# Where the columns of v are put in order: in the read of the matmul or in the copy out of PSUM

## The chip, the cores and the metric

One core of a Trainium2 chip. The metric is the device time of one execution in microseconds (us). In this kernel TensorE does its matmuls out of SBUF into PSUM; ScalarE and VectorE copy PSUM back to SBUF. In the profile PE is TensorE's matmul side, PEld its weight loads (they overlap: 98% and 85% of the span busy in the kernel before), ACT is ScalarE, DVE is VectorE, and L299 is line 299 of the kernel. "Stationary" is the operand that is loaded as weights, "moving" the one that is streamed past them.

## The reference, cut to what matters

```
q, k, v: (8 batches, 8 heads, 576 positions, 64)         fp32
kv  = einsum('bhsd,bhse->bhde', k, v)                     # 64 x 64 per batch and head
out = einsum('bhsd,bhde->bhse', q, kv)
x   = out / sqrt(mean(out^2, -1) + 1e-6) * g_norm          # then (4608, 512)
h   = x @ w_in (512 x 2048);  g = s * relu(h)^2 + b;  result = g @ w_out
```

The two large products at the end are nearly all of the work. The change concerns only `kv`, the k^T v product.

## The kernel before: the parts that matter here

The later part of the kernel wants the 64 columns of `kv` (index e of v) in the order "all e with e % 4 = 0, then 1, 2, 3". The kernel before gets this order for nothing in instructions: the moving operand of the matmul is v read every fourth element.

```
def kv_product(b):
    ps = [ps_t.tile([P, 2, D], FP32, name="kv_ps", tag="t") for _ in range(2)]
    for i in range(2):
        kv = kv_in.pop((b, i))
        for j in range(R):                     # R = 9
            for l in range(2):                 # l, r: the four 64x64 quarters of the array
                for r in range(2):
                    rows = slice(r * HB, r * HB + HB)
                    nc.tensor.matmul(
                        ps[r][l * HB : l * HB + HB, i, :].rearrange("p (c e) -> p c e", c=KC),
                        lhsT=kv[rows, 0, l, j, :],
                        rhs=kv[rows, 1, l, j, :].rearrange("p (e c) -> p c e", c=KC),
                        start=(j == 0), stop=(j == R - 1),
                    )
    for r in range(2):
        for l in range(2):
            ls = slice(l * HB, l * HB + HB)
            to = bd_kv[b % 2][ls, 2 * r : 2 * r + 2, ls]
            if b == 0 and l == 1:
                nc.vector.tensor_copy(out=to, in_=ps[r][ls])
            else:
                nc.scalar.copy(to, ps[r][ls])
...
```

(HB and D are 64, KC is 4.) So one batch is 2 x 9 x 2 x 2 = 72 calls of a 64 x 64 x 64 matmul and four copies of 64 x 128 elements. The traces hold two matmuls, each with its own weight load, for every such fp32 call: 144 a batch, 1152 in all. Matmuls are counted here as the traces count them, and the 144 of one batch are called a burst. Batch 0 is done at the start of the kernel, beside the first transfers; batches 1 to 7 are wedged one by one between the large matmuls.

## Time and profile before

| | before |
|---|---|
| time, median of the first 3 runs | 1001.62 us (1001.38 to 1002.2) |
| span of the profiled run | 1000.7 us |
| TensorE busy | 98% |
| k^T v matmuls (L299) on the chain that ended last | 3% |
| ScalarE, VectorE busy | 21%, 47% |

Read the chain first (which engine's work sets the end), then the groups of instructions by shape, then single bursts. The lines are in the prediction. One that it tells only in words is the copies after one burst, on ScalarE (columns: start us, duration us, engine, line, operation, operands, count, and in brackets the idle time before and who ended it):

```profile
176.25 1.07 ACT L313 COPY bd_kv<-kv_ps 64x128 f32<-64x128 f32 x4 [3.75 <-PE kv_ps L299]
```

The four copies start when the burst is over, and ScalarE had stood idle for 3.75 us by then: there is room for slower copies.

### The profile page before, as it was taken

Reading aid. Unit: us, or ns where it says so; the run is one execution under the profiler, and the core shown is the slowest. Engines: PE = TensorE matmul, PEld = TensorE weight load, DVE = VectorE, ACT = ScalarE, POOL = GpSimd, SP = SyncE. Lnnn points to the kernel's source line nnn. Section 1 sums busy time; section 2 is a strip of 40 time slices with the busy share of each in tenths; the row PEclk is TensorE's granted clock in tenths of the full one; section 3 lists DMA queues with packets and bytes.
Section 4 is the critical chain, followed back from the end, with each engine's and each line's share of the span. In section 5 each row is a group of like instructions: output and inputs, shape, how many; then the busy total and the mean of one; then the engine's idle time right before and its main releaser. Section 6 shows DMA issues by size and latency. Waiting matters only on the chain.

```text
span 1000.7 us, 15059 instructions
## 1 busy us (share of the span) xinstructions
PE 979.1 (98%) x6514; PEld 851.7 (85%) x6514; DVE 474.6 (47%) x777; ACT 208.7 (21%) x386; POOL 6.7 (1%) x18
## 2 busy tenths in 40 slices
PE   4999999999999999999999999999999999999998
PEld 3788888888888888888888888888888888888887
DVE  2689557453435444444345344533454444443441
ACT  2673131212220212121111212121112111212100
POOL 2000000000000000000000000000000000000000
PEclk9899999999999999999999999999999999999999
DMA  9688638522551344132442255125203240323033
GB/s 230 193 303 245 229 82 224 137 84 96 159 138 43 126 144 107 56 128 80 144 124 94 85 158 138 63 107 152 60 10 135 77 158 1 126 75 137 1 126 84
DMA packets 74225, 121.56 MB, mean 121 GB/s; under 512 B 41776, under 2 KB 47920, under 8 KB 66864
## 3 DMA queue, kind: packets, MB, share of 16 engines
q1 hardware_dynamic: 72208, 119.16, 39.0%
q10 hardware_dynamic: 1632, 1.44, 0.6%
q8 instruction: 51, 0.84, 0.3%
q14 instruction: 14, 0.11, 0.0%
q0 software_dynamic: 320, 0.00, 0.0%
HBM read 103.81 MB, written 16.78 MB: 121 GB/s over the span
## 4 chain that ended last, share of the span: by engine, by line
PE 94%; DVE 3%; DMA 2%; issue 0%; SPq 0%; ACT 0%; DVEq 0%; ACTq 0%
PE x_ps L84 48%; PE y_ps L84 30%; PE z_ps L84 8%; PE x_ps L345 3%; PE kv_ps L299 3%; PE qT_ps L331 1%; DMA kv_sb<-in_k_dram 1%; DMA q_sb<-in_q_dram 1%; DVE ws L186 1%; DVE xs L186 0%; DVE a L183 0%; DVE ws L183 0%; DVE a L437 0%; PE y_ps L345 0%; DVE wb L186 0%
## 5 line engine op out<-in xcount | busy, mean ns | idle before, releaser
L84 PE MATMUL x_ps<-w_sb,a 128*128 128x256 f32 x768 | 173.6, 381 | 0.0
L84 PEld LDWEIGHTS x_ps<-w_sb,a 128*128 128x128 f32 x768 | 144.6, 190 | 21.2 <-issue 2.8
L84 PE MATMUL y_ps<-w_sb,a 128*128 128x256 f32 x640 | 144.0, 381 | 0.0
L84 PEld LDWEIGHTS y_ps<-w_sb,a 128*128 128x128 f32 x640 | 120.3, 191 | 16.5 <-issue 1.4
L84 PE MATMUL x_ps<-xs,ws 128*128 128x256 f32 x512 | 121.2, 380 | 1.4 <-DVE ws L186 1.1
L84 PE MATMUL y_ps<-xs,wb 128*128 128x256 f32 x512 | 121.0, 380 | 0.0
L480 ACT COPY r<-x_ps 128x512 f32<-128x512 f32 x96 | 56.2, 585 | 298.3 <-PE x_ps L84 290.3
L84 PEld LDWEIGHTS x_ps<-xs,ws 128*128 128x128 f32 x512 | 97.4, 191 | 15.0 <-issue 1.5
L84 PEld LDWEIGHTS y_ps<-xs,wb 128*128 128x128 f32 x512 | 97.6, 191 | 13.0
L183 DVE TENSOR_TENSOR a<-y_ps,r 128x512 f32<-128x512 f32 x64 | 44.0, 688 | 122.1 <-ACT r L480 122.1
L84 PE MATMUL x_ps<-xT,wa 128*128 128x256 f32 x384 | 91.7, 387 | 0.0
L84 PEld LDWEIGHTS x_ps<-xT,wa 128*128 128x128 f32 x384 | 74.5, 195 | 10.8 <-ACT xT L384 0.4
L552 DVE SCALAR_TENSOR_TENSOR or<-x_ps,s_col,b_row 128x256 f32<-128x256 f32 x52 | 25.0, 483 | 94.5 <-PE x_ps L84 90.3
L437 DVE SCALAR_TENSOR_TENSOR a<-a 128x512 f32<-128x512 f32 x96 | 66.5, 692 | 3.3
L513 DVE TENSOR_TENSOR a<-a 128x512 f32<-128x512 f32 x32 | 22.1, 692 | 88.4 <-ACT a L512 88.4
L84 PE MATMUL x_ps<-xT,ws 128*128 128x256 f32 x256 | 61.1, 382 | 0.0
L84 PE MATMUL z_ps<-xT,wa 128*128 128x256 f32 x256 | 60.5, 380 | 0.0
L84 PE MATMUL x_ps<-w_sb,s 128*128 128x256 f32 x256 | 58.5, 382 | 0.0
L84 PEld LDWEIGHTS x_ps<-xT,ws 128*128 128x128 f32 x256 | 48.3, 190 | 7.3 <-issue 1.1
L84 PEld LDWEIGHTS z_ps<-xT,wa 128*128 128x128 f32 x256 | 48.8, 191 | 6.5
L84 PEld LDWEIGHTS x_ps<-w_sb,s 128*128 128x128 f32 x256 | 47.6, 190 | 7.2 <-issue 1.4
L356 DVE TENSOR_REDUCE ss<-xn 128x8 f32<-128x512 f32 x36 | 24.6, 684 | 52.9 <-ACT xn L354 52.2
(93 smaller groups left out, 855.8 us busy)
## 6 DMA issues: line engine op xcount, KB each, us to landing
w_sb<-w SPq DMA_DIRECT2D x56, 1024.0 KB, 4.9
out_dram<-o SPq DMA_DIRECT2D x72, 128.0 KB, 2.3
q_sb<-in_q_dram SPq DMA_DIRECT2D x70, 128.0 KB, 6.2
kv_sb<-in_k_dram SPq DMA_DIRECT2D x30, 288.0 KB, 5.1
kv_sb<-in_v_dram SPq DMA_DIRECT2D x30, 288.0 KB, 7.0
w_raw<-in_moe_w_in_dram SPq DMA_DIRECT2D x8, 1024.0 KB, 6.4
w_raw<-in_moe_w_out_dram SPq DMA_DIRECT2D x8, 1024.0 KB, 5.0
w<-w_up SPq DMA_DIRECT2D x3, 1024.0 KB, 6.9
```

The source lines that it names most:

```text
L84: nc.tensor.matmul(o, lhsT=lhsT, rhs=rhs, start=start, stop=stop, skip_group_check=True)
L183: nc.vector.tensor_tensor(out=o, in0=a, in1=b, op=ALU.add)
L186: nc.vector.tensor_tensor(out=o, in0=a, in1=b, op=ALU.subtract)
L299: nc.tensor.matmul(ps[r][l * HB : l * HB + HB, i, :].rearrange("p (c e) -> p c e", c=KC), lhsT=kv[rows, 0, l, j, :], rhs=kv[rows, 1, l, j, ...
L331: nc.tensor.transpose(ps[:, p, :], q_in[c][:, 2 * p : 2 * p + 2, :], ident)
L345: nc.tensor.matmul(ps[32 * p : 32 * p + 32, w, :], lhsT=st["qT"][:, p, 32 * w : 32 * w + 32], rhs=bd_kv[(b if w < 2 else b1) % 2][:, p, :] ...
L356: nc.vector.reduce_sum(st["ss"], st["xn"], axis=mybir.AxisListType.X)
L437: nc.vector.scalar_tensor_tensor(t, t, 0.0, t, ALU.max, ALU.mult)
L480: nc.scalar.copy(st[name], src)
L513: nc.vector.tensor_mul(t, t, t)
L552: nc.vector.scalar_tensor_tensor(o, ps, s_col, other, ALU.mult, ALU.add)
```

## The change

Its intent: let the matmul stream v as it lies in SBUF, and pay for the order where the result is small, in the copies that are made anyway.

```
                         nc.tensor.matmul(
-                            ps[r][l * HB : l * HB + HB, i, :].rearrange("p (c e) -> p c e", c=KC),
+                            ps[r][l * HB : l * HB + HB, i, :],
                             lhsT=kv[rows, 0, l, j, :],
-                            rhs=kv[rows, 1, l, j, :].rearrange("p (e c) -> p c e", c=KC),
+                            rhs=kv[rows, 1, l, j, :],
...
-                to = bd_kv[b % 2][ls, 2 * r : 2 * r + 2, ls]
+                to = bd_kv[b % 2][ls, 2 * r : 2 * r + 2, ls].rearrange("p i (c e) -> p i c e", c=KC)
+                src = ps[r][ls].rearrange("p i (e c) -> p i c e", c=KC)
                 if b == 0 and l == 1:
-                    nc.vector.tensor_copy(out=to, in_=ps[r][ls])
+                    nc.vector.tensor_copy(out=to, in_=src)
                 else:
-                    nc.scalar.copy(to, ps[r][ls])
+                    nc.scalar.copy(to, src)
```

## The prediction

The sum of the forecast came to 987.9 us: 1001.6 less seven bursts of 1.95 us (13.7 us). They are a paragraph that weighed such figures against the trace, the bound for the slower copies ("twofold" in rival 4 refers to it), and the paces that rivals 2 and 3 assumed, with the times worked out from them. The 0 for the copies stands as the author's estimate, from ScalarE's 21% and the 3.75 us that it idles in a burst. The upper end of the range, 998, was the time of rival 2, an assumption; the shift from 987.9 to 989 rests on the rivals likewise.

> **What bounds the kernel now.** I read the page from its head: busy shares, then the chain that ended last, then groups of instructions by shape, then the timeline around one k^T v product, and last the single records of that stretch.
>
> ```profile
> PE 979.1 (98%) x6514; PEld 851.7 (85%) x6514; DVE 474.6 (47%) x777; ACT 208.7 (21%) x386; POOL 6.7 (1%) x18
> PE 94%; DVE 3%; DMA 2%; issue 0%; SPq 0%; ACT 0%; DVEq 0%; ACTq 0%
> PE x_ps L84 48%; PE y_ps L84 30%; PE z_ps L84 8%; PE x_ps L345 3%; PE kv_ps L299 3%; PE qT_ps L331 1%; DMA kv_sb<-in_k_dram 1%; DMA q_sb<-in_q_dram 1%; DVE ws L186 1%; DVE xs L186 0%; DVE a L183 0%; DVE ws L183 0%; DVE a L437 0%; PE y_ps L3
> ```
>
> TensorE sets the time: 98% busy and 94% of the chain. The line that the change touches, L299, is 3% of the span (30 us) on that chain. This is the ceiling of the whole gain, before any mechanism.
>
> ```profile
> L345 PE MATMUL x_ps<-bd_kv,qT 128*32 128x128 f32 x1088 | 37.3, 278 | 1.6 <-DVE qT L334 1.1 <-DVE xn L364 0.5
> L299 PE MATMUL kv_ps<-kv_sb 64*64 64x64 f32 x1152 | 35.8, 293 | 10.2 <-DMA kv_sb<-in_v_dram 10.2
> L299 PEld LDWEIGHTS kv_ps<-kv_sb 64*64 64x64 f32 x1152 | 33.7, 157 | 12.6 <-issue 12.6
> L313 ACT COPY bd_kv<-kv_ps 64x128 f32<-64x128 f32 x30 | 7.7, 259 | 46.7 <-PE kv_ps L299 46.5
> ```
>
> A pair to notice: a matmul that streams 64 columns (L299) takes 293 ns, one that streams 128 columns (L345) only 278 ns. Half the columns should cost less.
>
> ```profile
> 171.50 0.38 PE L84 MATMUL x_ps<-xT,wa 128*128 128x256 f32 x1
> 171.81 4.41 PE L299 MATMUL kv_ps<-kv_sb 64*64 64x64 f32 x144
> 176.15 0.48 PE L84 MATMUL x_ps<-xT,ws 128*128 128x256 f32 x1
> ```
>
> One product is one burst of 144 matmuls, wedged between the large matmuls with no wait inside. First start to last start is 4.41 - 0.29 = 4.12 us, so 4.12/143 = 28.8 ns a matmul and 115 ns for a group of four, one in each 64x64 quarter of the array. In the single records the four start within about 20 ns, then nothing starts until about 115 ns after the first: each quarter is busy with its own stream, and issue isn't the limit.
>
> **How long should a stream of 64 columns be?** 16 of the 256-column matmuls take 3.45 us on the chain: 216 ns each, or 0.84 ns a column. The 128-column matmuls of L345 repeat on a column tile every 109 ns: 0.85 ns a column, with their own weight loads hidden. At that rate 64 columns take 54 ns, plus some 2 ns: 56. The trace shows 115, so 59 ns are unexplained, and the only thing peculiar to L299's moving operand is that v is read every fourth element (16 bytes apart). The strongest sign comes from batch 0, which ran before the clock had risen:
>
> ```profile
> L299 PEld LDWEIGHTS kv_ps<-kv_sb x144: 175/202/229, 8.6 to 14.7; 64*64 64x64 f32 x144
> L299 PE MATMUL kv_ps<-kv_sb x144: 290/293/367, 8.6 to 14.9; 64*64 64x64 f32 x144
> ```
>
> Against 129/151/154 and 290/291/306 for the burst at 171.8. The loads took 46 ns more at the minimum, roughly the 54 ns that a doubled stream of 64 columns would add, but the matmuls kept their 290 ns. I read it as half clock (the transposes that follow at 15.08 also come about 215 ns apart instead of 109; the page records no clock so early). A stream that doesn't slow when the array does isn't paced by the array but by its reads.
>
> [...]
>
> **The change, part by part.**
> - Removed: the strided read, in 8 x 144 = 1152 matmuls. The weights, the number of matmuls, the PSUM addresses written and the accumulation stay.
> - Array time after: 56 ns a group if the next weights load entirely beside the stream. A load of a 64-column weight also occupies about 53 ns (in the records the second group's loads follow the first's by 53 to 55 ns), and it begins 1 ns after the matmul whose slot it waits for. So loads and streams are now nearly equal in length and some friction is likely. I choose 62 ns, an estimate.
> - Per burst: 36 groups x (115 - 62) = 1.91 us, and the last matmul ends some 60 ns sooner, which shortens the hand-over to the next large matmul by perhaps that. Call it 1.95 us: 4.34 becomes about 2.4.
> - How many bursts count: batches 1 to 7 lie on the chain between large matmuls. Seven times 1.95 is 13.7 us. Batch 0 lies beside transfers, as the start of the chain shows:
>
> ```profile
> 2.44 8.87 DMA kv_sb<-in_k_dram
> 11.31 0.02 issue
> 11.32 0.58 SPq L135
> 11.90 0.04 issue
> 11.95 0.63 SPq L114
> 12.58 0.04 issue
> 12.62 8.68 DMA q_sb<-in_q_dram
> 21.30 0.14 issue
> 21.43 0.64 PE qT_ps L331 x4
> ```
>
> TensorE waits for q until 21.4 whatever batch 0 does at 8.6 to 15.1: gain 0.
> - Added: the stride in the copies out of PSUM. Same 32 instructions and bytes; [...] on an engine 21% busy, with no wait for bd_kv on ScalarE's copies anywhere in L345's idle time. For batch 0 two copies are on VectorE ahead of the copies of qT; [...] Cost on the path: 0.
> - Moved: TensorE reaches everything after each burst 2 us sooner. The one place where VectorE sets the pace, 148 to 168 us (the operand sums of the second unit), begins with a wait for TensorE at 147.6, so batch 1's gain passes through.
>
> Sum: 1001.6 - 13.7 = 987.9. I place the single number slightly up, at 989, because the rivals below all take from the gain.
>
> **Rivals.**
> 1. The stride isn't the cost; a weight load and a stream take turns in a quarter (54 + 54 + 7 = 115). For: the sum fits, and loads are stretched from 129 to 151 ns. Against: half clock would make it 215, and batch 0 shows 115 to 123. Time: 1001.6, no change.
> 2. Issue takes over: [...] For: no sustained rate above one in 27 ns is seen. Against: after a semaphore at 16.96 us the sequencer put out 13 loads and matmuls in 80 ns, 6 ns each, so a group of 8 would need 49. [...]
> 3. Loads and streams overlap badly once equally long[...]
> 4. The PSUM read is far slower than twofold, or VectorE or ScalarE becomes late for the next large group. Against: in each burst VectorE and ScalarE stop after their 0.5 to 0.7 us of leftovers and wait 3.75 us. Time: still under 1001.6 unless copies exceed 2 us each.
>
> **Range and chances.** Best case 56 ns a group and the short hand-over: 7 x (36 x 59 + 60) ns = 15.3 us, 986.3; runs before differed by 0.8 us. [...] So 8 in 10: 985.5 to 998. A gain over 2% needs 20 us off, more than two thirds of the 7 x 4.34 = 30.4 us that these bursts hold, a group in under 40 ns, shorter than its own stream; a loss over 2% needs a new wait of 20 us that nothing points to.
>
> **What would show it.** Right: L299's mean falls from 293 to about 220 ns (164 ns of fixed length, as in L345's 273 - 109, plus 56), the burst from 4.41 to about 2.5 us, its stretch on the chain from 3% to under 2%; large matmuls stay at 216 ns apart. Wrong by rival 1: the burst stays at 4.4. [...] By rival 4: [...]a new wait for bd_kv ahead of L345.

## The result, and the profile after

The changed kernel took 987.45 us (median of 4 runs, 986.9 to 988.22) against 1001.73 us (4 runs): ratio 0.9858, 95% interval 0.9841 to 0.9875. A ratio here is the mean time of one kernel's runs over the mean of the other's in the same rounds, so not quite the ratio of the medians. The gain is clear of noise and within 2%.

The page of the changed kernel (engines with busy us, share and instructions; then the chain by line):

```profile
PE 965.1 (98%) x6514; PEld 836.1 (85%) x6514; DVE 474.6 (48%) x777; ACT 208.8 (21%) x386; POOL 6.7 (1%) x18
PE x_ps L84 49%; PE y_ps L84 30%; PE z_ps L84 8%; PE x_ps L346 3%; PE kv_ps L299 2%; PE qT_ps L332 1%; DMA kv_sb<-in_v_dram 1%; DMA q_sb<-in_q_dram 1%; DVE ws L186 1%; ACT xT L385 0%; DVE xs L186 0%; DVE ws L183 0%; DVE a L183 0%; SPq L96 0
```

The same instructions in the same number; TensorE lost 14.0 us of busy time (15.6 us of its weight loads), the others none. On the chain L299 went from 3% to 2%. The groups by shape (busy us, mean ns, then idle before):

```profile
L299 PE MATMUL kv_ps<-kv_sb 64*64 64x64 f32 x1152 | 21.0, 231 | 10.8 <-DMA kv_sb<-in_v_dram 10.8
L299 PEld LDWEIGHTS kv_ps<-kv_sb 64*64 64x64 f32 x1152 | 19.7, 145 | 13.2 <-issue 13.2
L314 ACT COPY bd_kv<-kv_ps 64x128 f32<-64x128 f32 x30 | 7.7, 260 | 32.5 <-PE kv_ps L299 32.3
L312 DVE COPY bd_kv<-kv_ps 64x128 f32<-64x128 f32 x2 | 0.5, 290 | 0.7 <-ACT bd_kv L314 0.7
```

The matmuls' mean fell from 293 to 231 ns. The copies, which now read PSUM 16 bytes apart, take 260 ns against 259 on ScalarE and 290 against 290 on VectorE: the stride costs them nothing. The burst of batch 2 on the timeline:

```profile
169.69 0.38 PE L84 MATMUL x_ps<-xT,wa 128*128 128x256 f32 x1
170.00 2.35 PE L299 MATMUL kv_ps<-kv_sb 64*64 64x64 f32 x144
172.28 0.48 PE L84 MATMUL x_ps<-xT,ws 128*128 128x256 f32 x1
```

From the burst's first start to the first large matmul after it: 172.28 - 170.00 = 2.28 us, before 176.15 - 171.81 = 4.34.

Where the 14.3 us came from can be added up, because both traces hold the same matmuls in the same order. These are starts of the first large matmul after each burst (after batch 0, of the second group of 16), from the single records:

| after the burst of batch | before, us | changed, us | difference, us |
|---|---|---|---|
| 0 (second group of large matmuls) | 34.78 | 34.96 | +0.18 |
| 1 | 116.05 | 114.24 | -1.80 |
| 2 | 176.15 | 172.28 | -3.86 |
| 3 | 283.97 | 278.02 | -5.94 |
| 5 | 499.61 | 489.50 | -10.10 |
| 7 | 715.25 | 700.99 | -14.26 |
| last matmul of all | 995.95 | 981.69 | -14.26 |

Seven steps of 1.98 to 2.08 us, and nothing given back in the 280 us after the last burst. The first row is scatter of the start and no measure of batch 0: in after_again, the same kernel as the changed one, batch 1's burst starts at 110.53 us instead of 111.96. Counted from that burst's start to the last matmul the traces agree far better: 884.24 us before and 884.23 in only0, 869.72, 869.73 and 869.72 in the changed kernel, after_again and psum_write. The seven bursts are worth 14.51 us, 2.07 each.

### The profile page after: what moved, and what is told of

Its sections match the earlier page's. It is cut to its first block, busy times and chain, and to the rows that moved or that the text cites. A ratio compares the mean times of both kernels' runs of the same rounds, so it can differ in the third digit from the quotient of the medians.

```text
span 986.4 us, 15059 instructions
## 1 busy us (share of the span) xinstructions
PE 965.1 (98%) x6514; PEld 836.1 (85%) x6514; DVE 474.6 (48%) x777; ACT 208.8 (21%) x386; POOL 6.7 (1%) x18
## 4 chain that ended last, share of the span: by engine, by line
PE 93%; DVE 3%; DMA 2%; ACT 1%; issue 0%; SPq 0%; ACTq 0%; DVEq 0%
PE x_ps L84 49%; PE y_ps L84 30%; PE z_ps L84 8%; PE x_ps L346 3%; PE kv_ps L299 2%; PE qT_ps L332 1%; DMA kv_sb<-in_v_dram 1%; DMA q_sb<-in_q_dram 1%; DVE ws L186 1%; ACT xT L385 0%; DVE xs L186 0%; DVE ws L183 0%; DVE a L183 0%; SPq L96 0%; DVE xn L365 0%
```

## The experiments

They ran each on one chip, together with runs of the kernel before. "Spacing" is the time from one group of four matmuls to the next: four times (last start - first start)/143 in the burst of batch 3, from the single records. The records don't name the quarter of the array; that a group is one matmul in each quarter is read from the order of the calls.

| run | what is strided | spacing, ns | median, us | ratio to before (95%) |
|---|---|---|---|---|
| before | stream of v, 16 bytes | 115.2 | 1001.9 | |
| after_again | copies only | 59.0 | 987.7 | 0.9855 (0.9842 to 0.9869) |
| only0 | stream of v, batches 1 to 7 | 115.2 | 1002.06 | 0.9999 (0.9986 to 1.0011) |
| psum_write | write into PSUM | 59.0 | 987.69 | 0.9856 (0.9841 to 0.9871) |
| stride2 | stream of v, 8 bytes | 59.7 | 987.67 | 0.9856 (0.9842 to 0.9869) |
| stride8 | stream of v, 32 bytes | 116.4 | 1001.96 | 1.0001 (0.9984 to 1.0017) |
| half_plain | nothing, 32 columns | 58.2 | 986.93 | 0.9853 (0.9838 to 0.9867) |
| half_stride4 | stream of v, 16 bytes, 32 columns | 59.8 | 987.94 | 0.9862 (0.9847 to 0.9876) |
| k_strided | weights (k), 16 bytes | 118.6 | 1002.3 | 1.0006 (0.9991 to 1.0021) |

The theory under test: the matmul's stream was paced by reading elements 16 bytes apart. Its rivals: weight load and stream take turns; any gap costs; the cost only moves into PSUM; every burst counts alike.

**after_again.** The changed kernel, no edit.

> The changed kernel unchanged, for a tighter interval. All theories were made with its first result known: 987.5 us, ratio 0.986, bursts of 144 matmuls in 2.35 us.

Measured as expected; the interval of the ratio is now 0.9842 to 0.9869.

**only0.** Batch 0 alone is changed:

```
-                            rhs=kv[rows, 1, l, j, :],
+                            rhs=kv[rows, 1, l, j, :] if b == 0
+                            else kv[rows, 1, l, j, :].rearrange("p (e c) -> p c e", c=KC),
...      (the same choice for the place in PSUM and for the copies)
```

> Batch 0 alone reads v as it lies; batches 1 to 7 keep the strided read. Theory (batch 0 lies beside the transfer of q and counts nothing): within 0.1% of before, 1001.7 us, with the bursts of batches 1 to 7 at 4.4 us. Rival (every burst counts alike): one eighth of the gain, 1.8 us, about 999.9.

1002.06 us, ratio 0.9999. One eighth of the gain would be a ratio of 0.998, which lies outside the interval, 0.9986 to 1.0011, by a little. Batch 0 counts nothing that these runs can see: after it TensorE waits for q in both kernels (2.41 us before, 1.95 us in the changed one). The view by tile of batch 0 alone in only0 (weight loads, then matmuls; minimum/median/maximum ns, first and last start in us):

```profile
L299 PEld LDWEIGHTS kv_ps<-kv_sb x144: 175/223/228, 8.8 to 14.9; 64*64 64x64 f32 x144
L299 PE MATMUL kv_ps<-kv_sb x144: 311/311/364, 8.8 to 15.0; 64*64 64x64 f32 x144
```

This view also supports the prediction's reading of batch 0. Read as it lies, the stream takes 311 ns here and 218 ns later, so in these first 15 us the array is slow and a stream that the array paces is slow with it; the strided one was recorded at 290 ns in both places. That it was the clock is inferred, since the trace has no record of it there, from the kernel before: the transposes after batch 0 start 213 ns apart, and 110 ns apart from 16.41 us on, where the trace's first record of full clock begins (16.40). From 24.40 to 25.30 us, where the granted clock was 0.50, they start 213 ns apart again. By starts, which are measured and not modelled as the ends are: in the first 72 matmuls of batch 0, from the third group on, a group takes 115 to 121 ns before and 106 to 107 ns in only0; at full clock it takes 116 (before) and 58 (changed kernel). The slow clock nearly doubled the plain groups and hardly touched the strided ones.

**psum_write.** v is streamed as it lies, and the matmul's write into PSUM makes the order; the copies are the old ones:

```
-                            ps[r][l * HB : l * HB + HB, i, :],
+                            ps[r][l * HB : l * HB + HB, i, :].rearrange("p (c e) -> p e c", c=KC),
-                            rhs=kv[rows, 1, l, j, :],
+                            rhs=kv[rows, 1, l, j, :].rearrange("p (e c) -> p e c", c=KC),
...
-                src = ps[r][ls].rearrange("p i (e c) -> p i c e", c=KC)
+                src = ps[r][ls]
```

> v is read as it lies and the columns are put in order where the matmul writes PSUM (16 bytes apart in runs of 4 elements); the copies are those of before. Theory that only the read of v is slow: 987.5 us and 218 ns a matmul. Rival, [...]: groups of four near 115 ns, bursts near 4.4 us, about 1001.7 us.

(The distance in that text is wrong: consecutive results land 16 elements, 64 bytes, apart. The reason that it gave for the rival is cut: no run showed it.) The matmuls of one burst, in the view by tile:

```profile
L299 PE MATMUL kv_ps<-kv_sb x144: 218/218/267, 170.1 to 172.3; 64*64 64x64 f32 x144
```

The same as the changed kernel, in a correct result. A scattered write into PSUM is free here (59.0 ns a group with and without it), and so is the scattered read of the copies in the changed kernel (260 against 259 ns): the cost didn't move into PSUM, it went away. It was the read of SBUF alone. (A small slowing of the write could hide behind the weight load, but then the matmuls would be recorded longer, as in half_stride4 below; they kept 218 ns.)

**stride2 and stride8.** The stream of v every second, or every eighth element; the copies make up the rest of the order, so both results are correct.

```
 stride2
-                            ps[r][l * HB : l * HB + HB, i, :],
+                            ps[r][l * HB : l * HB + HB, i, :].rearrange("p (c e) -> p c e", c=2),
-                            rhs=kv[rows, 1, l, j, :],
+                            rhs=kv[rows, 1, l, j, :].rearrange("p (e c) -> p c e", c=2),
...
+                src = ps[r][ls].rearrange("p i (x h) -> p i h x", h=2)

 stride8: c=8 in the matmul, and
+                src = ps[r][ls].rearrange("p i (g c e) -> p i c e g", c=KC, g=2)
```

> v is read every second element (8 bytes apart[...]), the rest of the order is made in the copies; the result stays right. Theory [...]: groups at 58 ns, 987.5 us, as the changed kernel. Rival 1 (any gap between elements costs): groups at 115 ns, 1001.7 us. [...]

> v is read every eighth element (32 bytes apart); the result stays right. Theory [...] the same 115 ns a group, bursts of 4.4 us and 1001.7 us. Rival (cost grows with the distance): over 120 ns a group and over 1003 us.

(Cut from these two texts: the picture of what lies behind the cost, which no run showed, and a second rival to stride2 that rested on it.)

Two answers of the view by tile, the matmuls of one burst, stride2 and then stride8:

```profile
L299 PE MATMUL kv_ps<-kv_sb x144: 215/217/269, 169.5 to 171.7; 64*64 64x64 f32 x144
```

```profile
L299 PE MATMUL kv_ps<-kv_sb x144: 293/294/308, 171.5 to 175.7; 64*64 64x64 f32 x144
```

8 bytes apart costs what lying side by side costs (59.7 against 59.0 ns a group), 32 bytes apart costs what 16 bytes did (116.4 against 115.2). So it isn't "any gap", and hardly the distance: of the distances tried there is one step, between 8 and 16 bytes. What in the memory makes it was not shown.

**half_plain.** 32 of the 64 columns of v are streamed, weights as before. Its output is wrong, which doesn't matter for the time.

```
-                            ps[r][l * HB : l * HB + HB, i, :],
+                            ps[r][l * HB : l * HB + HB, i, : HB // 2],
-                            rhs=kv[rows, 1, l, j, :],
+                            rhs=kv[rows, 1, l, j, : HB // 2],
...                          (copies of 64 x 64)
```

> Wrong on purpose: only the first 32 columns of v are streamed, read as they lie; the weights keep their 64 columns. Which of the two paces a group at 58 ns now? If the weight load: groups stay at 55 to 58 ns, bursts near 2.3 us, about 987.5 us. If the stream: groups near 30 ns, bursts near 1.2 us, 7 x 36 x 28 ns = 7 us less, about 980.5 us.

The view by tile of one burst (weight loads, then matmuls; minimum/median/maximum ns):

```profile
L299 PEld LDWEIGHTS kv_ps<-kv_sb x144: 129/135/135, 169.3 to 171.4; 64*64 64x64 f32 x144
L299 PE MATMUL kv_ps<-kv_sb x144: 212/219/240, 169.3 to 171.4; 64*64 64x32 f32 x144
```

and the burst on the timeline:

```profile
169.28 2.33 PE L299 MATMUL kv_ps<-kv_sb 64*64 64x32 f32 x144
```

Half the stream, and the burst takes 2.33 us instead of 2.35: the stream no longer sets the pace. By the single records a slot of the group repeats every 58.3 ns in both kernels, with its parts differently placed: in the changed kernel a load starts 2 to 3 ns after the matmul before it and its matmul 56 ns later; in half_plain the load starts 30 ns after the matmul and its matmul 28 ns later. What stays is 58 ns from one load of 64 columns to the next, so the weight load is the likely pace-setter. No run has shorter weights, but three things speak for it: in the slow clock of batch 0 half_plain's groups take 107 ns, as 64 columns would at half speed (32 would take 54, an estimate from the 0.84 ns a column of the large matmuls); k_strided below makes the load longer and the group follows; and in the changed kernel nothing at all starts for 33 to 36 ns of each group of batch 3, so the issue of instructions isn't full.

**half_stride4.** 32 columns, every fourth element. Its output is wrong, which doesn't matter for the time.

```
+                            rhs=kv[rows, 1, l, j, :].rearrange("p (e c) -> p c e", c=KC)[:, :2],
...                          (32 places in PSUM; copies of 64 x 64)
```

> Wrong on purpose: 32 columns of v are streamed, every fourth element. Theory (the read of one element 16 bytes from the last takes about 1.77 ns and runs beside the weight load): 32 x 1.77 = 57 ns, groups at 57 to 60 ns, about 987.5 us. Rival 1 of the prediction (load and stream take turns, 54 + 27 + 7): 88 ns a group, about 995 us.

(The 1.77 ns are an estimate from the kernel before: 115.2 ns a group, less 2, over 64 elements.)

The same views:

```profile
L299 PE MATMUL kv_ps<-kv_sb x144: 229/236/248, 169.4 to 171.6; 64*64 64x32 f32 x144
```

and the burst on the timeline:

```profile
169.40 2.40 PE L299 MATMUL kv_ps<-kv_sb 64*64 64x32 f32 x144
```

59.8 ns a group, not 88. Load and stream don't take turns; they run side by side, and by these runs the longer one sets the pace (the stream at 115.2 ns in the kernel before, the load at 118.6 in k_strided). That rival is out. A limit of this run: since the load alone gives 58, it can't confirm the 57 ns of the stream; only the longer matmuls (236 against 219 ns) show that the strided read still costs, out of sight.

**k_strided.** Its output is wrong, which doesn't matter for the time. The weights are read every fourth element (64 elements are picked out of 256 of k):

```
-                            lhsT=kv[rows, 0, l, j, :],
+                            lhsT=kv[rows, 0, l].rearrange("p j d -> p (j d)")[:, 16 * j : 16 * j + 256]
+                            .rearrange("p (n s) -> p n s", s=4)[:, :, 0],
```

> Wrong on purpose: v as it lies, but the weights are read from k every fourth element over 256 elements. If the weight read pays as the stream did: loads last some 60 ns longer and groups take about 115 ns, 1001.7 us. If the weights' own read is free of it: loads stay at 135 ns, groups at 58 ns, 987.5 us. I expect the first.

Again one burst by tile:

```profile
L299 PEld LDWEIGHTS kv_ps<-kv_sb x144: 189/213/215, 171.1 to 175.2; 64*64 64x64 f32 x144
L299 PE MATMUL kv_ps<-kv_sb x144: 277/279/328, 171.1 to 175.3; 64*64 64x64 f32 x144
```

and the burst on the timeline:

```profile
171.06 4.52 PE L299 MATMUL kv_ps<-kv_sb 64*64 64x64 f32 x144
```

The loads last 60 ns longer at the minimum (189 against 129), a group takes 118.6 ns and the whole gain is gone. The read pays about the same whichever side of TensorE asks for it (115.2 ns a group for the stream, 118.6 for the weights). One estimate from these runs fits all spacings: a group takes the longer of its load and its stream, plus 2 to 6 ns, with 64 columns at 54 ns when plain or 8 bytes apart (64 times the 0.84 ns of the large matmuls) and about 113 ns when 16 or 32 bytes apart (from 115.2, 116.4 and 118.6).

No experiment points to a version that beats the changed kernel: psum_write and stride2 equal it, and as the product is cut here there is a weight load of 64 columns for every 64 columns of stream. Another cut of it wasn't tried.

## Why the prediction was right, point by point

- **The mechanism (the strided read paces the stream).** Shown: stride8 and the kernel before (116.4 and 115.2 ns a group) against stride2 and the changed kernel (59.7 and 59.0) put the step between 8 and 16 bytes; psum_write clears PSUM of it (59.0); k_strided makes the cost come back on the other operand (118.6).
- **62 ns a group.** Slightly too much: 58.3 ns in the steady part, 59.0 with the start of the burst. Seven bursts of 36 groups times 3.0 ns are 0.76 us. Of the 6 ns of friction that were added for equal loads and streams, 2 to 3 were found. The array time of 56 ns was close partly by luck: it is the stream's length, and the load, which likely sets the pace (half_plain), is as long (53 to 55 ns by the prediction).
- **The hand-over, 60 ns.** In the single records the large matmul after the burst of batch 2 starts 220 ns after the last small one before and 148 ns in the changed kernel: 72 ns.
- **1.95 us a burst, seven bursts, 13.7 us.** 2.07 us a burst and 14.51 us by the traces from batch 1's burst on, 14.28 us by the medians. The sum, 987.9, was nearer to 987.45 than the 989 that was then chosen out of regard for the rivals.
- **Batch 0 counts nothing.** Shown by only0, to within 0.11 to 0.14% of the time.
- **Copies, cost on the path 0.** They didn't grow at all (260 ns against 259). What an element takes is seen here: half_plain's copies of 64 elements took 207 ns, 53 ns less for 64 elements less, 0.83 ns each.
- **218 ns a matmul foretold as about 220, evenly in groups.** As measured; starts in a group lie 6 to 7 ns apart, so issue (rival 2) didn't take over: 288 loads and matmuls in a row went out at 7.4 ns each on average (59.0/8). Rival 1 fell with the changed kernel's 58.3 ns and with half_stride4, rival 3 with 58.3 ns, rival 4 with the copies (260 ns).
- **Batch 0's 290 ns as the strongest sign.** Those are durations, whose ends the profile models; the starts bear the argument out better than it was made (115 to 121 ns a group at what is read as half clock, 116 at full, against 107 and 58 for the plain read).
- **Slips that changed nothing.** The four of a group start within about 20 ns in batch 1's burst, but drift to 57 ns apart in the one that is shown (batch 2's). VectorE stops after 0.5 us in the other bursts, but works 2.75 us beside batch 1's. At 17.04 us 12 loads and matmuls went out in 78 ns, not 13 in 80. 20 of 30.4 us is just under two thirds.

## What to carry to other kernels

Compare groups of matmuls by columns streamed: if 64 columns take as long as 128 (here 115 ns against 109), look at how the operand is read before looking at waits. In these runs (fp32) neighbours of the moving stream 8 bytes apart in SBUF were free (59.7 against 59.0 ns a group) and 16 bytes apart cost double on both sides (115.2 moving, 118.6 stationary). Where the columns must be put in order, try it at PSUM, in the write or in the copy; both were free here (218 ns a matmul, 260 against 259 ns a copy). Then count only those bursts that lie on the chain, and ask what the next pace-setter is (here most likely the weight load, at half the old spacing).
